# Attention and two mixture layers on one core: every stage cut into single steps, buffers and banks given out by the source, and the order of all engines and transfers fixed for the whole program

## The chip, the core and the metric

The kernel runs on one core of one Trainium2 chip, in one launch. The metric is the device time of that core in microseconds (us). The core has five engines that each take their instructions strictly in the order in which the program lists them: TensorE (PE, whose weight loads are the separate row PEld), VectorE (DVE), ScalarE (ACT), GpSimd (POOL) and SyncE (SP), which in this kernel only starts transfers. An instruction starts when those ahead of it on its engine allow it and when the semaphores that it waits for have come.

## The reference

Inputs are fp32: x is 8 batches x 8 heads x 512 x 64, state is 8 x 8 x 32 x 64. Cut to what matters:

```python
def _attn_ref(x, state):
    scores = scale * np.matmul(x, state.transpose(0, 1, 3, 2))
    a = softmax(scores);   xread = np.matmul(a, state)
    scores2 = scale * np.matmul(state, x.transpose(0, 1, 3, 2))
    a2 = softmax(scores2); sread = np.matmul(a2, x)
    return np.concatenate([xread, sread], axis=2)
def _moe_ref(x, w_in, w_out, g_ln):      # 512 -> 1024 -> 512
    h = x @ w_in
    sm = softmax(h);  solu = h * sm
    ln = (solu - mean) / np.sqrt(var + 1e-06) * g_ln
    return ln @ w_out
def _moe2_ref(x, w_in, w_out):           # 512 -> 2048 -> 512
    h = x @ w_in
    return np.maximum(0.01 * h, h) @ w_out
```

The rows between are 8 x (512 + 32) = 4352 tokens of 512 values.

## The kernel before, in words

The program has three stretches.

**The attention and the first layer, batch by batch.** For each batch b: `load_x` brings x into the one buffer `xn` (four transfers), `load_state` brings the state into `z`. `at_xT` transposes x on PE (tile `xt`, token `T`), `at_state` the state (`zt`, token `Z`), `at_scores` multiplies (`st`, token `S`) and starts the second softmax, `at_soft1` makes the first one (`ee`, token `U`), `at_a2T` and `at_sread` read the state's side (`a2t` and `sr`, tokens `A` and `R`), `at_a1T` the other (token `B`). `sw` (token `Y`, later `W`) is the state multiplied into the first layer's weights. `h1` is the first layer for 128 rows (token `h`, bank pair `h`), which ends in `solu_norm` (tiles `e(b, r)` of 128x1024 and columns of 128x1), `tr` transposes its result (`tr`), `x2` multiplies by w_out (`x`). Products are made of three fp32r matmuls on high and low halves (`mm3`), in batches 0 and 1 partly of plain fp32 ones. Weights are loaded raw (`a`, `b`), narrowed on DVE (`i`, `o`) and split into halves (`j`, `p`: ACT makes the high half, POOL the low one; the low halves of w_out are the instructions of line 245).

**The second layer's first pair of 512-token blocks (pair 0)**, chunk by chunk of the 2048 columns. `split_chunk` (token `d`) narrows a chunk of weights on DVE and has POOL make its low halves (`w2`, `wo2`, `misc`) and the four sums `ws`. `h2` (token `H`, tiles `C`, `gb`, `gc`) makes the hidden layer by a scheme of seven products, `out2` the output (`o`), and `h8`/`out8` (tokens `K`, `Q`, tiles `c8`, `g8`) do the same for the 256 rows of the state.

**Pairs 1 to 3**, from about 600 us on, are written step by step in `rest()` from the three tables HEAD, PATTERN and TURN; there `kept()` ties every instruction to the one before it on its engine.

Outside `rest()`, the string PROGRAM lists whole stages, one token each, and `emit` maps a token's letter to its function. Each stage issues all its instructions at once. `MANUAL` is False, so the tile scheduler then moves instructions on each engine by its own rules. Buffers that turn over are handed out by the pools: four banks under the one tag `p1`, two bank pairs under `p2`, three rows of 128x1024 under `t4`, sixteen small columns under `sm`.

Of the kernel before, what the change touches and what calls it, by code (L numbers as in the profile page):

```python
# [1 line left out]

# [18 lines left out]
P = 128  # L21
# [17 lines left out]

@with_exitstack  # L40
def attn_solu_leaky_kernel(
# [14 lines left out]
    nc = tc.nc  # L56
# [22 lines left out]
    def bank(name):  # L79
        return ps.tile([P, 512], F32, tag="p1", name=name, bufs=4)  # L80
# [4 lines left out]
    def bank2(name):  # L85
        return psb[0].tile([P, 1024], F32, tag="p2", name=name, bufs=2)
# [4 lines left out]
    def small(name, n=1):  # L91
        return sb.tile([P, 4], F32, tag="sm", name=name, bufs=16)[:, :n]

    def row(name):
        return slot("t4", [P, 1024], F32, name, bufs=3)
# [4 lines left out]
    ordered = {}  # L100

    def kept(ins):

        if "on" in ordered:
            e, last = ins.ins.engine, ordered["on"]
            if e in last:
                tc.add_manual_dep(
                    ins.ins, last[e],
                    mybir.DependencyInfo(mybir.DependencyClass.NoSync, mybir.DependencyReason.DATA),
                    reason="order",  # L110
                )
            last[e] = ins.ins.name
        return ins
# [18 lines left out]
    make_identity(nc, ident)  # L132
# [118 lines left out]
    def at_state(b):  # L251
        for g in range(2):
# [3 lines left out]
            )  # L256
            for m in range(2):
                i = 1 + (m + b) % 2
# [4 lines left out]
                else:  # L263
                    split(stq[:, 0, 2 * g + m, d], stq[:, 1, 2 * g + m, d], pt[:, c])
# [11 lines left out]
    def at_xT(b, hp):  # L276
# [3 lines left out]
        for r in range(NR):  # L280
            nc.tensor.transpose(
                pt[:, r * P : (r + 1) * P], xn[:, r, hp * P : (hp + 1) * P], ident
            )
        hi, lo = att["xT_hi"][:, hp, :], xT_lo[:, hp, :]
        if b in PLAIN_S:
            nc.scalar.activation(hi, pt, AF.Copy, scale=SCALE)
            return
        nc.scalar.activation(hi, pt, AF.Copy, scale=SCALE)
        nc.vector.scalar_tensor_tensor(lo, pt, SCALE, f32(hi), ALU.mult, ALU.subtract)

    def at_scores(b, g):
        st = bank(f"st{b}_{g}")
        for m in range(2):
# [8 lines left out]
            )  # L302
        nc.vector.transpose(s1[:, g, :], st)
# [16 lines left out]
    def at_soft1(b, g):  # L320
# [941 lines left out]
```

## Time and profile before

| what | value |
|---|---|
| median of 3 runs | 1175.23 us (1174.89 to 1177.4) |
| the profiled execution | 1174.46 us |
| its span from first to last instruction | 1172.6 us |
| mean granted clock of TensorE | 0.994 |
| instructions recorded | 16515 |

The profiled execution is the span and 1.9 us around it; the median lies 0.8 us above it. Times within a view are counted from the span's start. A line number names the line of the kernel that issued the instruction; "idle before, releaser" is the time that the engine stood still just before and the instruction that ended it.

### The profile page before, as it was taken

To read this page: it belongs to the slowest core of one execution; us is meant where nothing else is said; L and a number is where in the kernel's file an instruction comes from. 1 tells how busy PE (TensorE), PEld (TensorE's weight loads), DVE (VectorE), ACT (ScalarE), POOL (GpSimd) and SP (SyncE) were. 2 spreads that over 40 slices of the span, in tenths; PEclk is the share of its full clock that TensorE was granted. 3 is DMA by queue.
4 is the path that set the end of the run, shared out by engine and by line. 5 is a ranking of instruction groups with operands and counts; after the bars stand their busy time and mean duration, and the time that the engine had idled before them with its cause. 6 is when DMAs were issued, how large, how long until landed. Compare 5 with 4: busy or idle time off the path is not lost.

```text
span 1172.6 us, 16515 instructions
## 1 busy us (share of the span) xinstructions
PE 1133.9 (97%) x6192; PEld 950.1 (81%) x6192; DVE 902.6 (77%) x1406; ACT 542.8 (46%) x907; POOL 546.8 (47%) x411
## 2 busy tenths in 40 slices
PE   4979999999999999989999999999999999999998
PEld 2554688888888888768888889999899998899997
DVE  6787686886886678658887787878977768867787
ACT  4674655665565545453333434434543334443331
POOL 3233111201102032767666475887767466655453
PEclk9998999999999999999999999999999999999999
DMA  9530512342162163655664477675877476665442
GB/s 297 181 74 10 151 75 57 101 126 64 41 176 79 48 260 124 244 185 200 221 229 138 178 284 264 232 289 205 299 285 286 181 280 244 243 239 215 163 189 73
DMA packets 88376, 211.85 MB, mean 181 GB/s; under 512 B 41320, under 2 KB 49512, under 8 KB 79080
## 3 DMA queue, kind: packets, MB, share of 16 engines
q1 hardware_dynamic: 88296, 210.79, 50.7%
q8 instruction: 49, 0.80, 0.3%
q14 instruction: 31, 0.25, 0.1%
HBM read 151.00 MB, written 59.77 MB: 180 GB/s over the span
## 4 chain that ended last, share of the span: by engine, by line
PE 48%; DMA 2%; POOL 2%; issue 2%; DVE 1%; ACT 1%; POOLq 0%; DVEq 0%; SPq 0%
PE hX L118 4%; PE hX L119 4%; PE hX L120 4%; PE oX L120 4%; PE oX L118 4%; PE oX L119 4%; PE o L120 2%; PE o L119 2%; PE o L118 2%; PE hY L118 2%; PE hY L119 2%; PE hY L120 2%; PE oY L120 2%; PE oY L119 2%; PE oY L118 2%
## 5 line engine op out<-in xcount | busy, mean ns | idle before, releaser
L947 DVE TENSOR_TENSOR oacc<-oacc,oX 128x512 f32<-128x512 f32 x171 | 116.0, 682 | 52.5 <-PE oX L120 50.4
L118 PE MATMUL x<-ln,w_out_hi 128*128 128x512 f32 (+1 forms) x256 | 96.9, 378 | 0.0
L120 PE MATMUL x<-ln,w_out_lo 128*128 128x512 f32 (+1 forms) x256 | 96.4, 376 | 0.0
L119 PE MATMUL x<-ln,w_out_hi 128*128 128x512 f32 (+1 forms) x256 | 96.3, 376 | 0.0
L881 ACT COPY C<-hX 128x512 f32<-128x512 f32 x72 | 42.2, 586 | 115.4 <-PE hX L120 115.3
L118 PE MATMUL hX<-xbT,w 128*128 128x512 f32 x192 | 76.4, 398 | 0.8 <-ACT C L881 0.7
L119 PE MATMUL hX<-xbT,w 128*128 128x512 f32 x192 | 75.8, 395 | 0.3 <-POOL xbT L756 0.3
L120 PE MATMUL hX<-xbT,w 128*128 128x512 f32 x192 | 75.0, 391 | 0.0
L910 POOL TENSOR_TENSOR gc<-C,gc 128x512 fp32r<-128x512 f32 x35 | 47.2, 1351 | 39.3 <-ACT gc L906 31.9
L947 DVE TENSOR_TENSOR oacc<-oacc,oY 128x512 f32<-128x512 f32 x93 | 63.1, 682 | 3.0 <-PE oY L120 2.2
L910 POOL TENSOR_TENSOR gb<-C,gb 128x512 fp32r<-128x512 f32 x35 | 48.0, 1376 | 34.3 <-PE oX L120 22.5
L889 DVE SCALAR_TENSOR_TENSOR C<-C 128x512 f32<-128x512 f32 x72 | 63.3, 880 | 0.4
L886 DVE TENSOR_TENSOR C<-C,hY 128x512 f32<-128x512 f32 x48 | 32.9, 686 | 31.9 <-ACT C L881 27.1
L119 PEld LDWEIGHTS x<-ln,w_out_hi 128*128 128x128 f32 x256 | 48.2, 188 | 8.8
L120 PEld LDWEIGHTS x<-ln,w_out_lo 128*128 128x128 f32 x256 | 48.2, 188 | 8.8
L118 PEld LDWEIGHTS x<-ln,w_out_hi 128*128 128x128 f32 x256 | 48.2, 188 | 8.7
L334 POOL TENSOR_TENSOR ee<-ee,sm 128x512 f32<-128x512 f32 x16 | 18.1, 1134 | 78.2 <-DVE sm L333 38.9
L910 POOL TENSOR_TENSOR gb<-S,gb 128x512 fp32r<-128x512 f32 x27 | 43.8, 1629 | 19.9 <-ACT gb L906 16.3
L910 POOL TENSOR_TENSOR gc<-S,gc 128x512 fp32r<-128x512 f32 x26 | 39.8, 1539 | 24.8 <-ACT gc L906 20.4
L128 DVE TENSOR_TENSOR ln<-tr,ln 128x512 fp32r<-128x512 f32 x60 | 39.0, 682 | 10.6 <-ACT ln L127 10.2
L120 PEld LDWEIGHTS hX<-xbT,w 128*128 128x128 f32 x192 | 36.1, 188 | 8.2
L118 PEld LDWEIGHTS hX<-xbT,w 128*128 128x128 f32 x192 | 36.3, 189 | 7.2 <-ACT C L881 1.1
(982 smaller groups left out, 3956.6 us busy)
## 6 DMA issues: line engine op xcount, KB each, us to landing
w<-w2s SPq DMA_DIRECT2D x24, 1792.0 KB, 11.2
shared<-wo2s SPq DMA_DIRECT2D x24, 768.0 KB, 4.3
wi<-wsc SPq DMA_DIRECT2D x14, 1024.0 KB, 5.4
xs<-xo SPq DMA_DIRECT2D x34, 256.0 KB, 2.4
raw<-in_moe_w_in SPq DMA_DIRECT2D x8, 1024.0 KB, 6.1
raw<-in_moe_w_out SPq DMA_DIRECT2D x8, 1024.0 KB, 6.0
w2s<-w SPq DMA_DIRECT2D x8, 1024.0 KB, 5.3
wo<-wt2s SPq DMA_DIRECT2D x8, 1024.0 KB, 6.4
```

The lines of the kernel that those rows point to most:

```text
L118: kept(nc.tensor.matmul(o, ah, bh, start=start, stop=False, **kw))
L119: kept(nc.tensor.matmul(o, ah, bl, start=False, stop=False, **kw))
L120: kept(nc.tensor.matmul(o, al, bh, start=False, stop=stop, **kw))
L128: nc.vector.tensor_tensor(lo, src, f32(hi), ALU.subtract)
L334: nc.gpsimd.tensor_tensor(e3, e3, sm.unsqueeze(2).to_broadcast([P, 16, NS]), ALU.mult)
L881: kept(nc.scalar.copy({"e0": a11, "e2": a21, "e4": a22}[tok], q["X"]))
L886: kept(nc.vector.tensor_tensor(v, v, q["Z" if tok == "z1" else "Y"], ALU.add))
L889: kept(nc.vector.scalar_tensor_tensor(v, v, 0.01, v, ALU.mult, ALU.max))
L910: kept(e.tensor_tensor(t[:, 1], src, f32(t[:, 0]), ALU.subtract))
L947: kept(nc.vector.tensor_tensor(d, d, v, ALU.add))
```

## The change

Stages become generators that `yield` between steps, and each token of PROGRAM (now some 2,200 of them) issues only the next step of its stage. A wrapper stands around all five engines and ties each instruction to the one issued before it on the same engine, for the whole program, so that the order of the source is the order that runs; before, this held in `rest()` alone. The buffers and banks that turn over are no longer handed out by the pools: `take` gives a number from a list of free ones, each number is a tag of its own with one buffer, and `drop` gives it back after the last use. The single columns of `solu_norm` and the softmaxes become columns of one tile each (`sn`, `sa`, `mx`, `my`), `solu_norm` of the last rows is a stage of its own (`N`), and `split_chunk` has its parts 0 to 5. The first chunk of pair 1 is issued by tokens with a "/" in front. On every engine the number of instructions is as before (PE 5976, DVE 1372, ACT 823, POOL 414, SP 344); what `rest()` issues is in the same order as before.

```diff
+class InOrder:
+    def __init__(self, tc, engine):
+        self.tc, self.engine, self.last = tc, engine, None
+    def __getattr__(self, name):
+        call = getattr(self.engine, name)
+        def issue(*args, **kw):
+            done = call(*args, **kw)
+            if PINNED and self.last is not None:
+                self.tc.add_manual_dep(
+                    done.ins, self.last,
+                    mybir.DependencyInfo(mybir.DependencyClass.NoSync, mybir.DependencyReason.DATA),
+                    reason="order",
+                )
+            self.last = done.ins.name
+            return done
+        return issue
...
-    def bank(name):
-        return ps.tile([P, 512], F32, tag="p1", name=name, bufs=4)
+    free = {"t": [0, 1, 2], "p": [0, 1, 2, 3], "P": [0, 1], "ln": [0, 1, 2, 3], "wi": [0, 1]}
+    held = {}
+    def take(ring, name, uses=1):
+        held[name] = [ring, free[ring].pop(0), uses]
+        return f"{ring}{held[name][1]}"
+    def drop(name):
+        held[name][2] -= 1
+        if not held[name][2]:
+            ring, k, _ = held.pop(name)
+            free[ring].append(k)
+    def bank(name, uses=1):
+        return ps.tile([P, 512], F32, tag=take("p", name, uses), name=name, bufs=1)
...
     def at_scores(b, g):
...
+        yield
         nc.vector.transpose(s1[:, g, :], st)
-        nm = small(f"nm2_{b}_{g}")
+        yield
+        sa = slot(f"sa{b % 2}{g}", [P, 4], F32, f"sa{b}_{g}")
+        nm = sa[:, 0:1]
         nc.vector.tensor_reduce(nm, st, AX.X, ALU.max, negate=True)
-        s2 = small(f"s2_{b}_{g}")
+        yield
+        s2 = sa[:, 1:2]
         nc.scalar.activation(a2[:, g, :], st, AF.Exp, bias=nm, accum_out=s2)
...
-    with tc.manual_schedule() if MANUAL else ExitStack():
-        for u in PROGRAM.split():
-            emit[u[0]](*(int(v) for v in u[1:].split(".") if v))
+    stages = {}
+    for u in PROGRAM.split():
+        if u not in stages:
+            stages[u] = stage(u)
+        if stages[u] is not None:
+            next(stages[u], None)
-MANUAL = False
+PINNED = True
...
-    a0 a1 x0.0 T0.0 a2 a3 x0.1 T0.1 z0. i0 T0.2 i1 T0.3 Z0 z1. S0.1 Z1 S0.0 Y1.0 i3 Y0.0 i2 b0
+    a0 i0 i0 i0 i0 i0 z0. Z0.1 a1 x0.0 T0.0 Z0.0 a3 i1 i1 i1 Z0.0 Z0.0 z1. i1 T0.0 i1 T0.1 T0.1
+    a2 S0.0 x0.1 i3 Z0.1 Z1.1 i2 Z1.1 Z0.1 T0.3 Z1.1 T0.2 Y0.0.0 i3 i3 i3 T0.3 z2. i2 i2 i2 T0.2
```

Three places show how the orders differ. First PE at the very start: before, its first instructions up to the first `sw` (the eight transposes of `xt0_0` and `xt0_1` and most of those of `xt0_2` and `xt0_3` stand ahead of these rows).

```order
L281 MATMUL xt0_3_188<-ident_75,xn_91 128x128
L254 MATMUL zt0_0_194<-ident_75,z0_83 128x128
L254 MATMUL zt0_1_198<-ident_75,z0_83 128x128
L124 MATMUL st0_1_206<-xT_hi0_146,stp_94 128x512 x2
L254 MATMUL zt1_0_218<-ident_75,z1_84 128x128
L254 MATMUL zt1_1_222<-ident_75,z1_84 128x128
L124 MATMUL st0_0_226<-xT_hi0_146,stp_94 128x512 x2
L124 MATMUL sw1_0_0_238<-sw0_169,stp_94 128x512 x2
```

After, the same engine from its first instruction on:

```order
L51 MATMUL zt0_1_152<-ident_75,z0_83 128x128
L51 MATMUL xt0_0_160<-ident_75,xn_91 128x128 x4
L51 MATMUL zt0_0_165<-ident_75,z0_83 128x128
L51 MATMUL xt0_1_181<-ident_75,xn_91 128x128 x4
L51 MATMUL st0_0_188<-xT_hi0_159,stp_94 128x512 x2
L51 MATMUL zt1_1_199<-ident_75,z1_84 128x128
L51 MATMUL xt0_3_205<-ident_75,xn_91 128x128 x4
L51 MATMUL xt0_2_211<-ident_75,xn_91 128x128 x4
L51 MATMUL sw0_0_0_216<-sw0_141,stp_94 128x512 x2
```

The state's transposes and the first scores `st0_0`, which need only half of x, now stand ahead of the transposes `xt0_2` and `xt0_3` of the other half; the state's transfers were moved ahead of that half too.

Second DVE at batch 1's second softmax, before: `r2` is the factor that scales `q4`, which PE transposes as `a2t`; `nm(0, 3)`, `sm1` and `ee1` belong to other stages.

```order
L305 TENSOR_REDUCE nm2_1_0_463<-st1_0_459 128x1
L438 TENSOR_SCALAR e(0, 0)_430<-e(0, 0)_430,c2(0, 0)_444 128x1024
L331 TENSOR_REDUCE sm1_1_566<-ee1_493 128x16
L309 TENSOR_SCALAR r2_1_0_467<-s2_1_0_465 128x1
L305 TENSOR_REDUCE nm2_1_1_481<-st1_1_477 128x1
...
L311 TENSOR_SCALAR q4_93<-q4_93,r2_1_0_467 128x512
L309 TENSOR_SCALAR r2_1_1_485<-s2_1_1_483 128x1
L415 TENSOR_REDUCE nm(0, 3)_511<-h0_3_506 128x1
L310 RECIPROCAL r2_1_1_485<-r2_1_1_485 128x1
L333 RECIPROCAL sm1_1_566<-sm1_1_566 128x16
L311 TENSOR_SCALAR q4_93<-q4_93,r2_1_1_485 128x512
```

After, with `sa1_0` and `sa1_1` as the tiles of the same columns:

```order
L51 STREAM_TRANSPOSE q4_93<-st1_0_419 128x512
L51 TENSOR_REDUCE sa1_0_436<-st1_0_419 128x1
L51 SCALAR_TENSOR_TENSOR e(0, 0)_422,sn(0, 0)_414<-h0_0_372,e(0, 0)_422 128x1024
...
L51 RECIPROCAL sa1_0_436<-sa1_0_436 128x1
L51 STREAM_TRANSPOSE q4_93<-st1_1_444 128x512
L51 TENSOR_REDUCE sa1_1_450<-st1_1_444 128x1
...
L51 TENSOR_SCALAR q4_93<-q4_93,sa1_0_436 128x512
L51 TENSOR_TENSOR ee1_454<-q4_93,mx1_1_455 128x512
...
L51 TENSOR_SCALAR sa1_1_450<-sa1_1_450 128x1
L51 RECIPROCAL sa1_1_450<-sa1_1_450 128x1
L51 TENSOR_SCALAR q4_93<-q4_93,sa1_1_450 128x512
```

Both maxima now come right behind their transposes, and `nm(0, 3)` and the scaling of `e(0, 0)` no longer stand among them.

Third POOL at the end of the first layer, before: `gb` and `gc` are the low halves of the hidden layer of pair 0, `g8_0` that of the state's rows, the others make weights of chunks 1 and 2.

```order
L849 TENSOR_TENSOR gb_3963<-C_3728,gb_3963 128x1024
L855 TENSOR_TENSOR gb_3963<-C_3728,gb_3963 128x1024
L590 TENSOR_TENSOR w2_0_1_4111<-wn1_0_4104,w2_0_1_4111 128x1024
...
L849 TENSOR_TENSOR gc_4125<-C_3728,gc_4125 128x1024
L855 TENSOR_TENSOR gc_4125<-C_3728,gc_4125 128x1024
L590 TENSOR_TENSOR w2_0_2_4357<-wn2_0_4350,w2_0_2_4357 128x1024
L1022 TENSOR_TENSOR g8_0_4259<-c8_0_4256,g8_0_4259 128x512
L601 TENSOR_TENSOR w2_0_2_4357<-ws2_4360,w2_0_2_4357 128x1024
```

After:

```order
L51 TENSOR_TENSOR gb_3743<-C_3538,gb_3743 128x1024
...
L51 TENSOR_TENSOR w2_0_1_3924<-ws1_3925,w2_0_1_3924 128x1024
L51 TENSOR_TENSOR misc_3964<-wn1_1_3839,misc_3964 128x1024
L51 TENSOR_TENSOR gb_3743<-C_3538,gb_3743 128x1024
...
L51 TENSOR_TENSOR g8_0_4109<-c8_0_4104,g8_0_4109 128x512
L51 TENSOR_TENSOR w2_0_2_4084<-ws2_4085,w2_0_2_4084 128x1024
L51 TENSOR_TENSOR gc_3975<-C_3538,gc_3975 128x1024 x2
```

`g8_0` now stands ahead of both `gc`, and weight work stands between the two `gb`.

## Rows read from the trace of the kernel before

**Rows 1.** The page's part 1: busy us (share of the span) xinstructions.

```profile
PE 1133.9 (97%) x6192; PEld 950.1 (81%) x6192; DVE 902.6 (77%) x1406; ACT 542.8 (46%) x907; POOL 546.8 (47%) x411
```

**Rows 2.** Stretches: us; busy of PE, PEld, DVE, ACT, POOL; clock; DMA share, GB/s.

```profile
9.00:29.00 20.00, 14.25 (x35) 6.60 (x36) 16.50 (x24) 10.63 (x23) 5.80 (x2) 1.00 0.94 305
29.00:117.00 88.00, 79.77 (x289) 45.40 (x288) 69.91 (x135) 53.25 (x96) 26.95 (x23) 0.94 0.30 89
117.00:469.00 352.00, 350.89 (x1804) 288.96 (x1803) 266.65 (x514) 201.25 (x362) 65.09 (x89) 1.00 0.34 108
469.00:541.00 72.00, 65.45 (x329) 54.18 (x328) 49.82 (x48) 33.33 (x44) 52.90 (x29) 0.98 0.64 220
600.00:1172.60 572.60, 564.55 (x3460) 505.59 (x3458) 451.07 (x632) 216.20 (x349) 352.32 (x237) 1.00 0.60 226
```

**Rows 3.** Waits of PE, 0 to 117 us: total, times, longest.

```profile
PE xt L281 <- DMA xn<-in_x: 14.0, 2, 9.0
PE a2t L343 <- DVE r L309: 3.4, 1, 3.4
PE st L119 <- DVE xT_lo L289: 2.4, 1, 2.4
PE st L124 <- ACT xT_hi L286: 1.6, 1, 1.6
PE tr L490 <- DVE e(0, 2)_627 L438: 0.7, 1, 0.7
```

**Rows 4.** Waits of PE, 469 to 541 us.

```profile
PE o L120 <- POOL g L1022: 3.1, 1, 3.1
PE o L118 <- ACT g L1021: 1.0, 1, 1.0
PE h L119 <- DVE misc L1002: 0.9, 1, 0.9
```

**Rows 5.** Three stretches at half clock, columns as in rows 2.

```profile
68.95:72.36 3.41, 3.41 (x16) 3.06 (x16) 3.41 (x6) 2.04 (x4) 1.14 (x1) 0.50 0.00 0
89.43:96.26 6.83, 6.14 (x19) 4.53 (x20) 4.86 (x6) 2.00 (x4) 6.70 (x3) 0.50 0.00 0
509.27:512.68 3.41, 2.88 (x7) 2.30 (x8) 2.94 (x2) 0.98 (x2) 2.80 (x2) 0.50 0.54 192
```

**Rows 6.** Timeline of PE: start, us, instruction [idle before <-releaser].

```profile
8.96 2.30 PE L281 MATMUL xt<-ident,xn 128*128 128x128 f32 x8 [8.96 <-DMA xn<-in_x]
...
16.27 2.45 PE L281 MATMUL xt<-ident,xn 128*128 128x128 f32 x8 [5.01 <-DMA xn<-in_x]
...
36.35 1.04 PE L343 MATMUL a2t<-ident,q 128*128 128x128 f32 x8
...
40.88 3.68 PE L355 MATMUL sr<-ee,xn 128*128 128x64 f32 x32
44.40 6.23 PE L124 MATMUL h<-sw,a1T 128*128 128x512 f32 x14
```

**Rows 7.** Issues of SP, 40 to 55 us, and their landing over 43 to 52 us.

```profile
43.93 2.94 SPq L171 DMA_DIRECT2D xn<-in_x  x4
xn<-in_x SPq DMA_DIRECT2D x4, 256.0 KB, 4.4
```

**Rows 8.** Timeline of DVE, 60 to 92 us.

```profile
68.68 1.22 DVE L415 TENSOR_REDUCE nm(0, 3)_511<-h 128x1 f32<-128x1024 f32 x1
78.97 0.80 DVE L438 TENSOR_SCALAR e(0, 3)_513<-e(0, 3)_513,c2(0, 3)_527 128x1024 f32<-128x1024 f32 x1
89.28 2.33 DVE L438 TENSOR_SCALAR e(0, 2)_627<-e(0, 2)_627,c2(0, 2)_641 128x1024 f32<-128x1024 f32 x1
```

**Rows 9.** Timeline of POOL, at 86 us and at the boundary.

```profile
86.39 9.74 POOL L245 TENSOR_TENSOR w_out_lo<-w_out_f,w_out_hi 128x1024 fp32r<-128x1024 f32 x4
503.82 2.37 POOL L855 TENSOR_TENSOR gc<-C,gc 128x1024 fp32r<-128x1024 f32 x1 [2.24 <-ACT gc L854]
...
508.46 1.28 POOL L1022 TENSOR_TENSOR g<-c,g 128x512 fp32r<-128x512 f32 x1
```

More of the change, by code (lines that the diff above doesn't have):

```diff
@@ L85, in bank2, with row @@
     def bank2(name):
-        return psb[0].tile([P, 1024], F32, tag="p2", name=name, bufs=2)
+        return psb[0].tile([P, 1024], F32, tag=take("P", name), name=name, bufs=1)
     def bank1(tag, name):
         return psb[0].tile([P, 512], F32, tag=tag, name=name, bufs=1)
[L91 to L95, printed above, removed]
+    def row(name, uses=1):
+        return slot(take("t", name, uses), [P, 1024], F32, name)
     xs = [dr.tile([P, ND, S if j < B else HALF], F32, name=f"xs{j}") for j in range(B + 1)]
[L100 to L113, printed above, removed]
     def mm3(o, ah, al, bh, bl, start, stop, more=False):
         kw = {"skip_group_check": True} if more else {}
-        kept(nc.tensor.matmul(o, ah, bh, start=start, stop=False, **kw))
-        kept(nc.tensor.matmul(o, ah, bl, start=False, stop=False, **kw))
-        kept(nc.tensor.matmul(o, al, bh, start=False, stop=stop, **kw))
+        nc.tensor.matmul(o, ah, bh, start=start, stop=False, **kw)
+        nc.tensor.matmul(o, ah, bl, start=False, stop=False, **kw)
+        nc.tensor.matmul(o, al, bh, start=False, stop=stop, **kw)
     def mm1(o, a, b, start, stop):
@@ L203, in load_w_in @@
         if k == 0:
-            raws["i"] = [slot("ln", [P, 2, FF, 2], U32, f"raw_in{i}", bufs=4) for i in range(2)]
+            raws["i"] = [slot(take("ln", f"raw_in{i}", 2), [P, 2, FF, 2], U32, f"raw_in{i}") for i in range(2)]
         nc.sync.dma_start(raws["i"][k // 2][:, k % 2], w_in[k * P : (k + 1) * P])
@@ L225, in load_w_out @@
         if k == 0:
-            raws["o"] = [slot("ln", [P, 2, 2 * DM, 2], U32, f"raw_out{i}", bufs=4) for i in range(2)]
+            raws["o"] = [slot(take("ln", f"raw_out{i}", 2), [P, 2, 2 * DM, 2], U32, f"raw_out{i}") for i in range(2)]
         nc.sync.dma_start(
@@ L380, in sw_of, with at_sw1 @@
         return sw[b]
-    def at_sw1(b, g):
-        for n in range(2):
+    def at_sw1(b, g, n):
+        for _ in (0,):
             c = slice(n * 512, (n + 1) * 512)
@@ L456, in h1 @@
                 )
-        solu_norm((b, r), hp_)
+        yield
+        yield from solu_norm((b, r), hp_)
     hs = []
     def h1s(k):
-        if k == 0:
-            hs.extend(bank2(f"hs{r}") for r in range(2))
         for r in range(2):
+            if k == 0:
+                if r:
+                    yield
+                hs.append(bank2(f"hs{r}"))
             for n in range(2):
@@ L725, in line @@
     def line(n, p):
-        return row(f"{n}_{p}").rearrange("p (k t) -> p k t", k=2)
+        return row(f"{n}_{p}", 2 if n in ("T1", "T2") else 1).rearrange("p (k t) -> p k t", k=2)
     def xpart(p, n):
@@ L917, in out2s @@
         new = n in ("A11", "S1") or (n == "A12" and c == 0)
-        if q == 0:
-            if n == "A12" and c == 0:
-                oq[p, tag] = [bank1(t, f"oz{p}_{t}") for t in "JZ"]
-            elif new:
-                oq[p, tag] = [bank(f"o{tag}{p}_{c}_{u}") for u in range(2)]
-        else:
+        if new:
+            u = f"o{tag}{p}_{c}_{q}"
+            oq[p, tag, q] = bank1("JZ"[q], u) if n == "A12" else bank(u)
+        if q:
             ring.append(a)
-        pt = oq[p, tag][q]
+        pt = oq[p, tag, q]
         for k in range(2):
@@ L991, in rows8 @@
         load_x8()
-        split_x8()
+        yield
+        yield from split_x8()
     def load_x8():
@@ L1118, in split_srs @@
         t = slot("q6", [P, 2, NHP, B * NS], F32R, "srs")
-        split(t[:, 0], t[:, 1], srT)
-        return t[:, 0], t[:, 1]
+        yield from split(t[:, 0], t[:, 1], srT)
+        srs.extend((t[:, 0], t[:, 1]))
     srs = []
@@ L1148, in attn_solu_leaky_kernel @@
         "d": split_chunk,
-        "s": lambda: srs.extend(split_srs()),
+        "s": split_srs,
         "D": first_x2,
         "E": second,
-        "H": lambda p, c, i: (h2(p, c, i), [step(t, p, c) for t in (AFTER.get(i, "") if p else "").split()]),
+        "H": h2,
         "O": out2,
```

583 lines of the change are left out of this document (407 added, 176 removed).

## The prediction

> **What bounds the kernel now.** I read the busy times first [rows 1]: PE has 97% of the span, the next engine 77%, so a gain can only come from time in which PE stands still or works slowly. The table of stretches [rows 2] says where that is. From 117 to 469 us PE is idle for 352.00 − 350.89 = 1.1 us: nothing is left there. From 600 us on it is idle for 572.60 − 564.55 = 8.1 us, but that part keeps its order. What is open lies at two places: the start (9.0 us before the first matmul [rows 6], 20.00 − 14.25 = 5.8 us from 9 to 29 us, 88.00 − 79.77 = 8.2 us from 29 to 117 us) and the boundary between the layers (72.00 − 65.45 = 6.6 us from 469 to 541 us).
>
> Then the waits, by name. In the start [rows 3] PE waits 14.0 us for x (9.0 and 5.0, the two idle times of [rows 6]), and 3.4 + 2.4 + 1.6 + 0.7 = 8.1 us for DVE and ACT: the first 3.4 us before `a2t` of batch 1, 2.4 us before the scores of batch 2, 1.6 us before those of batch 1, 0.7 us before a `tr`. At the boundary [rows 4] it waits 3.1 us for POOL's `g`, 1.0 for ACT's `g` and 0.9 for `misc`, 5.0 us in the rows shown. Last the clock: at the 3.4, the 2.4 and the 3.1 us wait, from just ahead of their end on, PE runs at 0.50, its lower level of 1.2 GHz, for 3.41, 6.83 and 3.41 us [rows 5], 1.00 (2.4 GHz) around them. Matmuls at half clock do half the work, so these stretches cost about half their PE time: 3.41/2 + 6.14/2 + 2.88/2 = 6.2 us.
>
> So the most that an order could return is 9.0 + 5.8 + 8.2 + 6.6 + 6.2 = 35.8 us without what `rest()` holds; the 9.0 us are the first transfers themselves, which leaves 26.8 us.
>
> **The change part by part.**
>
> *Tying each instruction to the one before.* Engines run their lists in order anyway, and counts are equal on all five, so the ties themselves are worth nothing: no instruction is added that could cost, and the merged columns only join tiles. What is bought or sold is the order. From 600 us on it is unchanged: 0 there. What I put at nothing there is covered as before by PE's 564.55 us of work.
>
> *The start, 0 to 29 us.* The scores `st0_0` and the first state transposes now run between the two halves of x, in the 5.0 us [rows 6] in which PE stood still. That is about 2 matmuls of 128x512 in plain fp32; by the fourteen of [rows 6] (6.23/14 = 0.45 us a record, two records each) 4 records or 1.8 us, with some transposes (1.04/8 = 0.13 us each) about 2.4 us filled. Against it, eight state transfers now go ahead of the second half of x. They are small, and each issue holds SP for about 2.94/4 = 0.74 us [rows 7]. If the issues were the limit the second half would come 6 us later, but the DMA share is 0.94 in that stretch [rows 2], so it is the bytes that count, and these are few: I take 1 us late. Bounds −4 to +4, value +1.5.
>
> *29 to 117 us.* The wait of 3.4 us: the last scaling of `q4` came behind the maximum `nm(0, 3)`, 1.22 us [rows 8], and behind a scaling of `e(0, 0)` (0.80 by its like [rows 8]) and two operations on `ee1`/`sm1` (0.7 each, by the same engine's 128x512 forms, which I read as a bit under the 0.80). Out of order's way that is 1.22 + 0.80 + 1.4 = 3.4 us ahead of it: the wait goes. The second and fourth waits (2.4 and 0.7) come from POOL. At 86.39 us POOL begins four subtractions of w_out one after the other, 9.74 us [rows 9], and inside them the scaling of `e(0, 2)` takes 2.33 us where its like takes 0.80 [rows 8]. In the new order these four stand as one, two and one with other stages between, so that no DVE run is stretched three times in a row. The Trainium skill, "SBUF — State Buffer", section "Who interferes with whom", says that GpSimd and VectorE share one port pair as an exclusive lock, and that the loser blocks entirely; the 2.33 us against 0.80 agree with it. By that rule a move does not remove the 9.74 us of overlap, it only picks other victims. That is the ground of the rival below on POOL; in the sum, the 2.4 + 0.7 count in full. The 1.6 us for ACT's `xT_hi`: the new order puts the transposes of `xt1` together instead of spread over `h0`, with `st1_0` soon behind the two that it needs, so part of the wait stays; I count half, 0.8. Sum 3.4 + 2.4 + 0.7 + 0.8 = +7.3, bounds 0 and 8.2 (all of the stretch's idle time). Where the stall goes: DVE, with 69.91 of 88.00 us busy [rows 2], is next; 18 us of slack lie spread over the stretch, so the wait need not come back, but it may.
>
> *The clock.* Two of the three half-clock stretches lie in the start, just behind the 3.4 us and the 2.4 us waits [rows 3, 5]. If those waits go I take the clock to stay up: 3.41/2 + 6.14/2 = 4.8 us, of which I count 4.6. Bounds 0 and 4.8.
>
> *The next x.* `xn` has one buffer, so x of a batch can only be fetched when the last `sr` of the batch before has read it. In the kernel before, the four transfers started with `sr` running (40.88 to 44.56 us [rows 6]; issues 43.93 to 46.87, landing 4.4 us after issue [rows 7]), so x is there about 46.87 + 4.4 = 51.3 us at the latest, some 6 to 7 us behind the last `sr`. In the new order PE has, between the last `sr` and the first `xt` of the next batch, in batch 1 the transposes and the `h1_2` and half `h1_0`, 12 records at 0.45 = 5.3 us and 13 transposes at 0.13 = 1.7 us, 7.0 us in all; for the other batches I counted 6.5 to 15. That is just covered. Cost 0, and if the cover is gone a microsecond or two in each of seven batches.
>
> *117 to 469 us.* It has 1.1 us idle: nothing to win, and a hand-set order may make new waits. Bounds −10 and +1, value −3.
>
> *The boundary.* POOL is the engine waited for. There the low half `g8_0` (1.28 us) came behind `gc` (2.37) and `w2_0_2` (2.36, the time between the two rows less waits) [rows 9], and PE stood for 3.1 us [rows 4]. In the new order `g8_0` stands ahead of both `gc`. That takes 2.37 us at least from its start, and its consumer `o` stands later on PE too: 3.1 + 1.0 + 0.9 = 5.0 us, and the 2.88/2 = 1.4 us of the third half-clock stretch [rows 5]. `gc` behind it is 2 x 2.4 us later in POOL's list by one 1.28 us operation, and its first use on PE comes some 9 us after. I count +6.5 (6.4 summed, and 0.1 of smaller waits). Bounds −3 and +8.
>
> **Sum:** 1.5 + 7.3 + 4.6 − 3 + 6.5 = 16.9 us. The profiled execution of before took 1174.46 us (span 1172.6 and 1.9 around it), so 1157.6 us. The median of the runs is 0.8 us above the profiled one; on that scale **1158.3 us**. A measurement of this kernel can tell about 0.2%, 2.4 us, from no change; 16.9 is seven times that.
>
> **The rivals.**
>
> *Half of it, chance 0.20.* DVE is the limiter one step below PE: in 29 to 117 us it is busy for 69.91 us in a fixed list. If each wait that goes comes back shorter at the next thing PE needs from DVE, or one of the four POOL subtractions stretches another DVE run on PE's path by the same 1.5 us, start and boundary return half of 1.5 + 7.3 + 4.6 + 6.5 = 19.9 us, less 1.5 for new waits: 1175.2 − 8.5 = 1166.7. For it: 88.00 − 69.91 = 18 us of slack is spread thin. Against it: PE's waits there are four single events, not a steady lag.
>
> *No difference, 0.07.* The order as printed moves, but what PE waits for is the same data through the same chain, and the clock falls at other places. Then 1175. Against it: the 9.74 us of POOL in one piece is plainly split.
>
> *Slower, by the x cover, 0.07.* One place: the fetch of the next x behind the last `sr`. If it takes 9.5 us instead of the 6 to 7, because the new order sends more before it in the queue, PE stands 2.5 us in each of seven batches = 17.5 us, which eats the 16.9; a clock that falls after each (3.41/2 = 1.7 us, seven times 12) makes it 1175.2 − 16.9 + 17.5 + 12 = 1188. The point from which it decides is 9.5 us of fetch; [rows 7] shows 7.4 from the first issue. Before has no wait for x behind 29 us, which is against it.
>
> *More, 0.05.* The start hides nearly all of the 5.0 us and 117 to 469 us loses nothing: 1175.2 − 26.8 = 1148.5.
>
> **How the numbers follow.** The forecast, a gain of 12 to 23 us, has 0.61. Its own range is 1152 to 1164. The half-gain case takes the upper end to 1168, the greater gain the lower to 1148; left out are no difference, slower, and the tails: about 0.2. Range 1148 to 1168. Faster by over 0.2%: 0.61 + 0.20 + 0.05 = 0.86; within: 0.07; slower: 0.07.
>
> **What would show it.** Right: PE's first wait for x of 9 us stays, the second is shorter; no wait of PE above 1 us from 29 to 117 us, and clock 1.00 throughout; POOL's subtractions of w_out apart, and DVE's scalings of `e` at 0.8 us; no wait of `o` for POOL's `g`; waits from 117 to 469 us below 4 us; everything behind pair 1's start as long as before. Wrong: a `xt` in some batch that waits for DMA; PE waiting for DVE in many short pieces; idle time from 117 to 469 us above 10 us.

## The result and the profile after

The changed kernel takes 1156.14 us (median of 4 runs, 1155.37 to 1157.69), the kernel before 1175.06 in the same session: a ratio of 0.9836, 95% interval 0.9819 to 0.9853. The forecast was 1158.3 us, with 1148 to 1168 as the range. The profiled execution took 1156.16 us; its span is 1154.4 us, 18.2 less than before. Recorded instructions all carry line 51 now, the wrapper's call, so groups are read by their tiles.

The table of stretches of the changed kernel, columns as in [rows 2]. Places in the program come 16 to 18 us earlier behind the boundary, so its stretches end at 453, 523 and 582 us where those of before ended at 469, 541 and 600:

```profile
0.00:9.00 9.00, 0.44 (x1) 0.18 (x1) 1.76 (x3) 2.44 (x3) 3.87 (x11) 1.00 0.84 274
9.00:29.00 20.00, 17.84 (x45) 8.36 (x46) 19.24 (x28) 12.94 (x26) 3.15 (x1) 1.00 1.02 337
29.00:117.00 88.00, 87.75 (x346) 50.99 (x345) 76.76 (x154) 59.62 (x111) 23.12 (x24) 1.00 0.36 112
117.00:453.00 336.00, 334.07 (x1732) 278.33 (x1731) 259.30 (x488) 191.86 (x345) 69.13 (x88) 1.00 0.35 105
453.00:523.00 70.00, 70.00 (x379) 60.44 (x378) 41.92 (x47) 36.01 (x50) 44.55 (x26) 1.00 0.57 192
...
582.00:1154.40 572.40, 559.83 (x3413) 498.28 (x3411) 450.79 (x634) 214.88 (x347) 354.43 (x236) 1.00 0.62 233
```

Idle time is the stretch less PE's busy time. From 29 to 117 us it fell from 8.2 to 0.25 us, at the boundary from 6.6 to 0. From 0 to 29 us it is 8.56 + 2.16 = 10.7 us; before it was 9.0 + 5.8 = 14.7. In the last stretch it rose, from 572.60 − 564.55 = 8.1 us to 572.40 − 559.83 = 12.6: a loss that the prediction did not have.

The waits of PE over the whole program, the three largest:

```profile
PE zt L51 <- DMA z<-in_state: 6.9, 1, 6.9
PE xt L51 <- DMA xn<-in_x: 5.3, 5, 2.3
PE oX L51 <- POOL gc L51: 3.4, 2, 3.1
```

Nothing of [rows 4] is left, and of [rows 3] only the wait for the first transfers, now spread over `zt` and `xt`, and 0.2 us of the 1.6 for `xT_hi`. Of the five waits for x four, 3.3 us, lie in the start, and one, 1.9 us, in batch 4. New is 3.1 us before an `oX` that waits for POOL's `gc`. The clock is at its lower level in one stretch behind that wait, where [rows 5] showed three; this is the table of stretches for it:

```profile
699.51:702.92 3.41, 3.41 (x13) 2.83 (x12) 2.67 (x3) 0.45 (x1) 3.41 (x3) 0.50 1.07 449
```

How the new wait comes about is read in two timelines of the changed kernel, POOL's and SP's:

```profile
682.85 1.74 POOL L51 TENSOR_TENSOR gb<-C,gb 128x512 fp32r<-128x512 f32 x1
693.14 0.74 POOL L51 TENSOR_TENSOR wd<-wf 128x256 f32<-128x256 f32 x1 [8.55 <-DMA wf<-wf2s]
...
697.26 2.95 POOL L51 TENSOR_TENSOR gc<-C,gc 128x512 fp32r<-128x512 f32 x2
```

```profile
678.20 0.34 SPq L51 DMA_DIRECT2D out<-oacc  x1
680.51 0.32 SPq L51 DMA_DIRECT2D wt2s<-misc  x1
681.11 0.57 SPq L51 DMA_DIRECT2D out<-oacc  x1
681.78 0.84 SPq L51 DMA_DIRECT2D wf<-wf2s  x1
```

POOL stands for 8.55 us until `wf` lands at 693 us, then makes four sums `wd` of it, and only then `gc`, for which PE waits. SP issues that `wf` last, behind the last output rows of pair 0 and a store of weights, each of which first waits for its data. SP's timeline of the kernel before at the same work has it the other way round:

```profile
677.44 1.63 SPq L638 DMA_DIRECT2D wf<-wf2s  x1
...
688.90 0.34 SPq L988 DMA_DIRECT2D out<-oacc  x1
```

There only what `rest()` issues was tied, and this load is the first transfer of it; the scheduler was free to place pair 0's output rows behind it.

### The profile page after: what moved, and what is told of

Its sections match the earlier page's. It is cut to its first block, busy times and chain, and to the rows that moved or that the text cites. A ratio compares the mean times of both kernels' runs of the same rounds, so it can differ in the third digit from the quotient of the medians.

```text
span 1154.4 us, 16468 instructions
## 1 busy us (share of the span) xinstructions
PE 1128.9 (98%) x6192; PEld 945.8 (82%) x6192; DVE 895.7 (78%) x1406; ACT 540.7 (47%) x907; POOL 540.2 (47%) x411
## 4 chain that ended last, share of the span: by engine, by line
PE 89%; DMA 4%; DVE 3%; issue 1%; POOL 1%; ACT 0%; POOLq 0%; SPq 0%; DVEq 0%; ACTq 0%
PE x L51 17%; PE hX L51 14%; PE oX L51 10%; PE h L51 10%; PE o L51 8%; PE hY L51 7%; PE oY L51 5%; PE hZ L51 3%; PE tr L51 3%; PE sr L51 2%; PE oZ L51 2%; PE st L51 2%; PE sv L51 1%; DVE C L51 1%; PE sw L51 1%
## 5 line engine op out<-in xcount | busy, mean ns | idle before, releaser
L51 PE MATMUL x<-ln,w_out_hi 128*128 128x512 f32 (+1 forms) x512 | 153.8, 384 | 0.0
L51 PE MATMUL hX<-xbT,w 128*128 128x512 f32 x576 | 149.9, 395 | 1.5 <-ACT C L51 1.2
L51 PE MATMUL h<-sw,a1T 128*128 128x512 f32 x352 | 103.6, 436 | 0.0
L51 POOL TENSOR_TENSOR gc<-C,gc 128x512 fp32r<-128x512 f32 (+1 forms) x43 | 69.3, 1614 | 50.2 <-ACT gc L51 25.5
L51 POOL TENSOR_TENSOR gb<-C,gb 128x512 fp32r<-128x512 f32 (+1 forms) x43 | 69.8, 1629 | 45.9 <-ACT gb L51 23.6
L51 DVE SCALAR_TENSOR_TENSOR C<-C 128x512 f32<-128x512 f32 (+1 forms) x88 | 82.7, 940 | 0.6
L51 PEld LDWEIGHTS h<-sw,a1T 128*128 128x128 f32 x352 | 64.1, 188 | 23.2 <-issue 11.0
L51 DVE TENSOR_TENSOR oacc<-oacc,o 128x512 f32<-128x512 f32 x70 | 45.7, 681 | 21.6 <-PE o L51 21.3
L51 ACT CAST ln<-tr 128x512 fp32r<-128x512 f32 x60 | 34.5, 588 | 35.3 <-PE tr L51 35.2
L51 PE MATMUL hX<-xbB,w 128*128 128x512 f32 x192 | 50.9, 401 | 0.0
L51 PE MATMUL hY<-xbB,w 128*128 128x512 f32 x192 | 49.7, 394 | 0.4 <-DVE C L51 0.4
```

Of the source, the lines that this page charges most:

```text
L51: done = call(*args, **kw)
```

## The experiments

All are the changed kernel with the edit shown; the last has the two edits before it together. Tokens are given as they stand in PROGRAM, and lists are cut to the lines that change. Times are medians, to be held against 1156.1 us. Runs of one kernel lie 2 to 6 us apart here, so a difference of about 3 us is read from the trace and not from the time alone.

**Ties taken away, wholly and in part.**

```diff
-PINNED = True
+PINNED = False
```

> The changed kernel without the ties: steps, buffers and banks as in the change, but the scheduler may move instructions again on every engine (on DVE and SP its order then differs in most places). If the order is what pays and ties are free, as the prediction has it, the gain goes back in large part: 1165 to 1176 us. Rival: the division into steps and the buffers given out by the source carry the gain, and the scheduler keeps close enough to the source: 1155 to 1159 us.

Measured: 1241.96 us, 1.0572 (1.0557 to 1.0586) of before. Both expectations were too low by far. The two largest waits of PE:

```profile
PE hX L51 <- ACT C L51: 11.7, 5, 5.8
PE o L51 <- DVE oacc L51: 11.6, 5, 3.8
```

Since this also frees the part from pair 1 on, which was tied before the change, a second kernel keeps ties there alone:

```diff
     def rest():
+        global PINNED
+        PINNED = True
+        for n in vars(nc).values():
+            n.last = None
...
-PINNED = True
+PINNED = False
```

> The changed kernel with ties in the part written step by step alone, as before the change; steps, buffers and banks ahead of it as in the change, in the scheduler's order. Theory: fixed order ahead of that part is the whole gain, and what the scheduler makes of the divided source there costs at least as much as before: 1172 to 1185 us (the kernel without any tie lost 17 us more of PE's time than the changed one up to 560 us, and some of the clock). Rival: steps and buffers carry a part of the gain: 1158 to 1168 us.

Measured: 1206.57 us, 1.026 (1.0244 to 1.0277), again above both expectations. So the changed source without its order ahead of pair 1 is 31 us slower than the kernel before, and that order is worth 50 us on top of it. Which of the steps, the buffers and the new list of tokens the scheduler does badly with, no run separates. The table of stretches shows that the loss against the changed kernel lies at the start and, most of it, from 453 to 640 us, where PE is idle for 8.9 and 12.0 us and the clock's mean falls to 0.97 and 0.96:

```profile
29.00:117.00 88.00, 79.75 (x300) 45.21 (x300) 79.87 (x152) 60.37 (x108) 35.34 (x29) 0.96 0.31 94
...
453.00:560.00 107.00, 98.06 (x512) 83.37 (x511) 76.09 (x74) 49.19 (x67) 63.93 (x36) 0.97 0.54 187
560.00:640.00 80.00, 68.03 (x316) 55.61 (x314) 54.64 (x63) 28.06 (x36) 49.35 (x29) 0.96 0.53 179
```

**The start undone.** z goes behind x again, with what uses it.

```diff
-    a0 i0 i0 i0 i0 i0 z0. Z0.1 a1 x0.0 T0.0 Z0.0 a3 i1 i1 i1 Z0.0 Z0.0 z1. i1 T0.0 i1 T0.1 T0.1
-    a2 S0.0 x0.1 i3 Z0.1 Z1.1 i2 Z1.1 Z0.1 T0.3 Z1.1 T0.2
+    a0 i0 i0 i0 i0 i0 a1 x0.0 T0.0 a3 i1 i1 i1 i1 T0.0 i1 T0.1 T0.1 a2 x0.1 i3 i2 T0.3 T0.2 T0.3
+    T0.2 z0. z1. Z0.1 Z0.1 Z0.1 Z0.0 Z0.0 Z0.0 Z1.1 Z1.1 Z1.1 S0.0
```

> The changed kernel with the old start: the state's eight first transfers go behind the second half of x, and the state's transposes and st0_0 behind the transposes of x. The prediction's term of 1.5 us for the new start makes this 1157.6 us. Rival, by the idle time of PE from 0 to 29 us in the two traces (14.7 us before, 10.7 after): the start was worth 4 us, 1160 us.

Measured: 1159.29 us (1155.95 to 1161.43), 3.2 us more, with ranges that overlap; the span is 2.7 us longer. Its wait for x from 0 to 40 us is about what it was before the change, against 6.9 us for the state and 3.3 for x with the new start:

```profile
PE xt L51 <- DMA xn<-in_x: 13.4, 2, 8.9
```

What the start is worth is read better from the time at which PE reaches the first `sr` of batch 0, here, in the changed kernel and in the one with x of batch 4 first (further down):

```profile
36.60 1.89 PE L51 MATMUL sr<-ee,xn 128*128 128x64 f32 x16
32.58 1.89 PE L51 MATMUL sr<-ee,xn 128*128 128x64 f32 x16
36.26 1.89 PE L51 MATMUL sr<-ee,xn 128*128 128x64 f32 x16
```

The last two have the same order on every engine up to there. So have the eight other kernels below that keep all ties, and over these ten the time lies between 32.58 and 36.26 us, 34.5 in the mean. It goes with how long PE waits for the second half of x and whether the clock falls behind that wait: in eight of the ten profiles it is at its lower level there, for 3.4 us in six and for 6.8 in two. The profile of the changed kernel is one of the two without. For the slowest of the ten, the wait and the row of the table of stretches:

```profile
19.19 2.56 PE L51 MATMUL xt<-ident,xn 128*128 128x128 f32 x8 [3.04 <-DMA xn<-in_x]
```

```profile
18.16:24.99 6.83, 5.80 (x13) 2.94 (x14) 5.64 (x8) 2.65 (x6) 0.00 (x0) 0.50 0.74 236
```

So the start is worth between 0.3 and 4.0 us, about 2 in the mean, against the one profile of the old start. The rival's 4 is the gain of the fastest start of the ten, and these runs don't tell the sum's 1.5 from 3.

**The 3.4 us wait before `a2t`: PE's list or DVE's?** First PE's alone, `h0_3` behind the transposes:

```diff
-    o0 h0.3 S1.0 U1.1 Z2.1 U1.0 U1.1 h0.0 h0.3 S1.1 h0.1 S1.1 U1.0 U1.0 h0.1 A1.0 A1.0 A1.1 A1.1
+    o0 S1.0 U1.1 Z2.1 U1.0 U1.1 h0.0 S1.1 h0.1 S1.1 U1.0 U1.0 h0.1 A1.0 A1.0 A1.1 A1.1 h0.3 h0.3
```

> The changed kernel with one move on PE alone: the four matmuls of h0_3 go behind the transposes a2t of batch 1 instead of ahead of them; DVE's list stays. The prediction says that the wait of 3.4 us went because DVE's list no longer holds nm(0, 3) and the scalings ahead of the last scaling of q: then PE waits nothing here, 1156 us. Rival: PE's own list covers the wait with h0_3; DVE's last scaling ends at 56.9 us in the profile and PE would be there at about 54.1: a wait of 2.8 us, and a stretch at half clock behind it for 1.7 us more: 1159 to 1161 us.

Measured: 1159.11 us (1157.28 to 1160.99), as the rival has it. PE's timeline has the wait again, in two pieces, with no half clock behind it:

```profile
57.97 0.30 PE L51 MATMUL a2t<-ident,q 128*128 128x128 f32 x1 [0.74 <-DVE q L51]
59.99 0.98 PE L51 MATMUL a2t<-ident,q 128*128 128x128 f32 x7 [1.72 <-DVE q L51]
```

Then DVE's alone. A first try delayed the scaling behind its readers, so that `a2t` read `q` before its last scaling:

```diff
-    S1.1 U1.0 U1.0 h0.1 A1.0 A1.0 A1.1 A1.1 h0.0 j1 t0.0.0 t0.0.0 U1.1 U1.1 h0.2 h0.1 t0.1.0 h0.3
+    U1.0 U1.0 h0.1 A1.0 A1.0 A1.1 A1.1 h0.0 j1 t0.0.0 t0.0.0 U1.1 U1.1 h0.2 h0.1 t0.1.0 h0.3 S1.1
```

> The changed kernel with one move on DVE alone: the last scaling of q of batch 1 goes behind the maximum nm(0, 3) and what stands before it, about 4.2 us of DVE work later; PE's list stays, which reaches these transposes 0.6 us after the scaling ends now. The prediction's step: a wait of about 3.6 us comes back, with up to 1.7 us for the clock: 1160 to 1161.5 us. Rival: PE's list has enough room behind (softmax chains run ahead of need), and nothing comes back: 1156 to 1157 us.

Measured: 1155.5 us (1155.15 to 1158.56). With the dependency gone there was nothing to wait for, so this run tells nothing on the question. The second try brings the other work forward instead:

```diff
-    h0.1 S1.1 U1.0 U1.0 h0.1 A1.0 A1.0 A1.1 A1.1 h0.0 j1 t0.0.0 t0.0.0 U1.1 U1.1 h0.2 h0.1 t0.1.0
-    h0.3
+    h0.1 h0.1 h0.0 U1.1 h0.1 h0.3 S1.1 U1.0 U1.0 A1.0 A1.0 A1.1 A1.1 j1 t0.0.0 t0.0.0 U1.1 h0.2
+    t0.1.0
```

> The changed kernel with one move on DVE alone: ahead of the last scaling of q of batch 1 now stand the maximum nm(0, 3), the scalings of e(0, 0) and e(0, 1) and the sum of ee, about 4.1 us of work; PE's list stays, which reaches these transposes 0.6 us after the scaling ends now. The prediction's step (DVE's list alone made the wait): a wait of about 3.5 us comes back, with up to 1.7 us for the clock: 1159.5 to 1161.5 us. Rival: nothing comes back, since the chain runs ahead of PE's need: 1156 to 1157 us.

Measured: 1160.76 us (1158.28 to 1161.62), in the range of the prediction's step. PE's timeline and, below it, the stretch behind the wait, at half clock:

```profile
62.19 0.98 PE L51 MATMUL a2t<-ident,q 128*128 128x128 f32 x7 [2.79 <-DVE q L51]
```

```profile
63.50:66.80 3.30, 3.30 (x5) 1.21 (x5) 1.05 (x3) 2.29 (x4) 2.04 (x2) 0.50 0.00 0
```

So either move alone brings a wait of 2.5 to 2.8 us. In the new order both are needed: DVE's list is shorter ahead of the last scaling, and PE has `h0_3` to do meanwhile. That is not yet how the old wait came about; see the next section.

**POOL's four subtractions in one piece.** Four more of the same size, which the output does not need, at the place where they stood before the change:

```diff
+    def pool4():
+        w = raws["w"][:, 0:2, :]
+        for _ in range(4):
+            nc.gpsimd.tensor_tensor(w_out_lo[:, 6:8, :], w, w, ALU.subtract)
...
-    T2.2 o3 T2.0 t0.3.1 h0.2 t0.3.0 T2.0 h0.2 t0.2.0 T2.1
+    T2.2 o3 T2.0 t0.3.1 h0.2 t0.3.0 T2.0 h0.2 t0.2.0 T2.1 !
```

> The changed kernel with four subtractions of 128x1024 more on POOL, one after the other (9.7 us of work that the output does not need), ahead of the transposes of batch 2, where four of them stood in one piece before the change. The prediction's step (this piece made the waits of 2.4 and 0.7 us, by what it does to DVE): waits of about 3 us come back, and up to 3 us of clock: 1159 to 1162 us. Rival: what removed the waits is the order of PE and DVE there, and POOL's piece costs under 1 us: 1156 to 1157 us.

Measured: 1158.37 us (1157.41 to 1163.44), between the two expectations; the traces decide. The timelines of POOL, DVE and PE:

```profile
71.98 8.55 POOL L51 TENSOR_TENSOR w_out_lo<-w_out_f 128x1024 fp32r<-128x1024 f32 x4
```

```profile
72.51 1.47 DVE L51 TENSOR_SCALAR sn(0, 2)_535<-sn(0, 2)_535 128x2 f32<-128x2 f32 x1
74.01 2.46 DVE L51 TENSOR_SCALAR e(0, 2)_564<-e(0, 2)_564,sn(0, 2)_535 128x1024 f32<-128x1024 f32 x1
```

```profile
76.62 0.63 PE L51 MATMUL tr<-ident,e(0, 2)_564 128*128 128x128 f32 x4 [2.14 <-DVE e(0, 2)_564 L51]
```

Inside POOL's piece the scaling of `e(0, 2)` takes 2.46 us (0.81 in the changed kernel), much as the 2.33 of [rows 8], and PE waits 2.1 us for it; 3.4 us at half clock follow. Of the two waits of before the `tr` one came back, larger; that of `st` for `xT_lo` did not.

**The boundary's 3.1 us wait.** POOL's list alone, `g8_0` (the last K0 step) behind the first `gc` and `w2_0_2`:

```diff
-    K0 d2.0.3 K0 H0.1.5 d2.0.1 O0.0.1.1 K1 K1 K1 H0.2.0 H0.2.1 Q0.0 H0.2.0 H0.1.6 H0.2.1 d2.1.0
-    d2.0.3 d3.0.0 H0.2.2 Q0.1 O0.0.0.0 d2.0.4 d2.0.5 H0.1.5
+    K0 d2.0.3 H0.1.5 d2.0.3 H0.1.5 K0 d2.0.1 O0.0.1.1 K1 K1 K1 H0.2.0 H0.2.1 Q0.0 H0.2.0 H0.1.6
+    H0.2.1 d2.1.0 d3.0.0 H0.2.2 Q0.1 O0.0.0.0 d2.0.4 d2.0.5
```

> The changed kernel with POOL's old order at the boundary: g8_0 stands behind the first gc and the low half of w2_0_2, 4.8 us of POOL work later; PE's list stays. The prediction gave the 3.1 us wait and 1.4 us of clock to POOL's order: then 1160.6 us. Rival: PE's list, which uses g8_0 only 4.2 us after POOL has it, removes the wait by itself: a wait of 0.6 us at most, 1156 to 1157 us.

Measured: 1158.83 us, with wide runs (1156.34 to 1162.14), so the time falls between the expectations. The profiled execution is the fastest of the five; its span, 1154.6 us, is that of the changed kernel, and of the boundary's wait this came back:

```profile
PE o L51 <- POOL g L51: 0.8, 1, 0.8
```

POOL's and PE's list together, with the first `o8_0` (Q0.0) ahead of `h8_1`, `hX` and `hZ` as well:

```diff
-    H0.1.5 K0 d2.0.1 O0.0.1.1 K1 K1 K1 H0.2.0 H0.2.1 Q0.0
+    H0.1.5 K0 Q0.0 d2.0.1 O0.0.1.1 K1 K1 K1 H0.2.0 H0.2.1
```

> The changed kernel with both halves of the boundary's wait undone: g8_0 behind the first gc and the low half of w2_0_2 on POOL, and the first o8_0 ahead of h8_1, hX and hZ on PE. Theory: POOL's and PE's order each give cover (4.8 us and 5.6 us of work against 4.2 us of slack now), and only with both gone does a wait come back: about 6 us, with up to 1.7 us for the clock: 1161 to 1164 us. Rival: other work slides in and no more than 1 to 2 us come back: 1157 to 1158 us.

Measured: 1164.39 us (1160.68 to 1167.01), 8.3 us more, at the upper end of the theory. The wait, in the slowest of the six runs:

```profile
PE o L51 <- POOL g L51: 6.2, 1, 6.2
```

So it was not POOL's order by itself; PE's later use covers almost all of POOL's 4.8 us.

**The new wait at 699 us.** `wf2` is issued before the last output rows:

```diff
     def load_wf(c):
+        if c in wf:
+            return
...
-    Q7.0 /7.uc /8.V /8.m6
+    Q7.0 /7.uc /8.V /9.U /8.m6
```

> The changed kernel with one transfer moved: the load of wf2 is issued before the last output rows of pair 0 instead of behind them. Theory: the new wait of 3.1 us at 699 us and the half clock behind it come from fixed order on SP, which puts these output rows (and what they wait for) ahead of wf2; then 3.1 + 1.7 us go, 1151.4 us. Rival: the transfer is late because the DMA is busy, or POOL's sums are late for another reason: 1155 to 1157 us.

Measured: 1152.26 us (1151.57 to 1155.17), 0.9813 (0.9799 to 0.9828) of before, 3.9 us less than the changed kernel, and no run of the one lies in the range of the other. SP issues the load 4.4 us earlier, and POOL's sums are done before `gc` is wanted; the wait of 3.1 us and the half clock behind it are gone. SP and POOL in the trace of this run, which is the slowest of the four:

```profile
677.33 2.67 SPq L51 DMA_DIRECT2D wf<-wf2s  x1
682.12 0.34 SPq L51 DMA_DIRECT2D out<-oacc  x1
```

```profile
690.84 0.75 POOL L51 TENSOR_TENSOR wd<-wf,wd 128x256 f32<-128x256 f32 x1
695.90 1.29 POOL L51 TENSOR_TENSOR gc<-C,gc 128x512 fp32r<-128x512 f32 x1 [4.32 <-ACT gc L51]
```

**The wait for x of batch 4.** In the changed kernel PE's transposes wait once behind the start for x. Its timelines of PE and SP there:

```profile
181.15 1.20 PE L51 MATMUL xt<-ident,xn 128*128 128x128 f32 x9 [1.93 <-DMA xn<-in_x]
```

```profile
165.68 0.92 SPq L51 DMA_DIRECT2D wi<-wsc  x2
168.84 7.42 SPq L51 DMA_DIRECT2D xn<-in_x  x4
```

Two reloads of 1 MB go just ahead of x, and x takes 181.15 − 168.84 = 12.3 us from the first issue to the use of the last piece. The edit moves them behind it (`x4.` is unchanged; only its neighbours shown):

```diff
-    X1.2 w2.0 B3.0 B3.0 w2.1 h2.3
+    X1.2 B3.0 B3.0 h2.3
...
-    t2.0.0 x4. Z5.0
+    t2.0.0 x4. w2.0 w2.1 Z5.0
```

> The changed kernel with two transfers moved: the reloads of two first-layer weights (1 MB each) go behind the four transfers of x of batch 4 instead of ahead of them. Theory: they are why batch 4's transposes wait 1.9 us for x; then 1154.2 us. Rival: the reloads are then late for the state's product of batch 2 and the wait only changes its place: 1156 us or more.

Measured: 1155.36 us (1154.25 to 1157.19). No wait for x is left behind the start, nor one for the reloads; the time is 0.8 us less, which these runs can't tell from none. The profiled execution is even 1.0 us longer than that of the changed kernel: it is the one whose start came out 3.7 us later, as shown above.

**Both moves of transfers.**

> The changed kernel with both moves of transfers, wf2 early and x of batch 4 first. If both theories hold the gains add: 3.1 + 1.7 + 1.9 us, 1149.5 us, faster than both kernels. If either falls, 1151 to 1156 us.

Measured: 1152.27 us (1149.46 to 1152.86), 0.9804 (0.979 to 0.9818) of before: faster than both kernels, and equal to the one with `wf2` alone within the spread. Both waits are gone in its trace, but the 1149.5 us of the added gains did not come; its profiled execution has 3.4 us at half clock in the start. That the move of x is worth something in time is not shown.

## Why the prediction was right, and where its terms were not

The total, 1156.1 against 1158.3, and the sign are right, and so are the places of the gains. The terms err more than the total. In span, from the two profiles:

| term | predicted | measured | how |
|---|---|---|---|
| start, 0 to 29 us | +1.5 | +4.0 | idle 14.7 to 10.7; by the first `sr` 0.3 to 4.0 over ten profiles |
| waits, 29 to 117 us | +7.3 | +8.0 | idle 8.2 to 0.25 |
| 117 us to the boundary | −3 | −0.8 | idle 1.1 to 1.9 |
| boundary, waits | +5.1 | +6.6 | idle 6.6 to 0 |
| clock, three stretches | +4.6 and +1.4 | +5.0 | PE busy 1133.9 to 1128.9, the new stretch included |
| from pair 1 on | 0 | −4.5 | idle 8.1 to 12.6 |

The measured column adds up to 18.3, the span's 18.2. Two errors cancel: the gains were put 6 us too small in sum, and a loss of 4.5 us, with 1.7 us of half clock counted in the clock's row, was left out. That the total comes within 2.2 us is in part luck.

**The step that failed** is "From 600 us on it is unchanged: 0 there". The order of what `rest()` issues is unchanged, but not what stands ahead of it on SP; and `rest()` begins only with the load of `wf2`, so the first chunk of pair 1 ahead of it got a new order too. Tying the whole program put pair 0's output rows in front of `wf2`; the run with the load moved shows that cause, and that it cost 3.9 us. Of the 4.5 us of idle time 3.1 are this wait; the rest is in pieces below 1 us, which no run takes apart. The prediction asked what is queued on SP for the start and for x, but not here, and took unchanged work in a stretch for unchanged waits.

**The start.** I counted 2.4 us filled and 1 us lost. PE filled more: the four records of `st0_0` took 3.75 us, not 1.8, at a granted clock of 1.00, where those of `st0_1` took 1.88 a little later.

```profile
12.86 3.75 PE L51 MATMUL st<-xT_hi,stp 128*128 128x512 f32 x4 [0.17 <-issue]
21.40 1.88 PE L51 MATMUL st<-xT_hi,stp 128*128 128x512 f32 x4
```

Time filled by slow work is not all gained, and the half clock that most of the profiles have behind the second half of x was no term of the sum. By the ten profiles +1.5 is within what the start is worth.

**The wait of 3.4 us** was forecast to go, and went, but its lines were misread. The prediction added up what stands ahead of the last scaling of `q4`, `nm(0, 3)` included. PE's and DVE's timelines of the kernel before:

```profile
68.85 0.58 PE L343 MATMUL a2t<-ident,q 128*128 128x128 f32 x2 [3.35 <-DVE r L309]
69.22 1.91 PE L490 MATMUL tr<-ident,e(0, 0)_430 128*128 128x128 f32 x8
70.93 1.49 PE L343 MATMUL a2t<-ident,q 128*128 128x128 f32 x6
```

```profile
65.52 0.81 DVE L438 TENSOR_SCALAR e(0, 0)_430<-e(0, 0)_430,c2(0, 0)_444 128x1024 f32<-128x1024 f32 x1
...
68.22 0.48 DVE L311 TENSOR_SCALAR q<-q,r 128x512 f32<-128x512 f32 x1
...
68.68 1.22 DVE L415 TENSOR_REDUCE nm(0, 3)_511<-h 128x1 f32<-128x1024 f32 x1
...
70.03 0.46 DVE L311 TENSOR_SCALAR q<-q,r 128x512 f32<-128x512 f32 x1
```

The wait ended at 68.85 us, behind the first scaling, which is done at 68.70; `nm(0, 3)` and the last scaling come later. The transposes that need the last scaling stand behind eight `tr` on PE and did not wait. So what made the wait stands ahead of 68.22 us, the scaling of `e(0, 0)` and three reductions of 0.68 us among it, and that the prediction's sum is 3.4 too is luck. In the new order nothing stands on PE between the transposes of the two halves, so that the last scaling counts there; undoing PE's or DVE's part brings 2.5 or 2.8 us of wait and costs 3.0 or 4.6 us. The prediction named DVE's list alone. The same holds for **the boundary**: POOL's list undone alone returns a wait of 0.8 us, together with PE's 6.2. The prediction did mention the later use on PE, but rested the term on POOL. (The 2.36 us that it gives for `w2_0_2` is 2.27 by its two rows.)

**POOL's piece** was right in mechanism. The Trainium skill, "SBUF — State Buffer", section "Who interferes with whom", gives GpSimd and VectorE an exclusive port pair, and limits it to some VectorE instructions, `tensor_scalar` in its two-port modes among them and `tensor_reduce` not. The 2.46 us against 0.81 for the same scaling beside a piece of 8.55 us agree with it, and so does a reduction that takes 1.23 us in that piece as without it. The prediction left the limit out when it said that a move only picks other victims. That rival did not come: in the changed kernel no wait of PE behind DVE from 29 to 117 us is left. Only the `tr` part of the two waits was reproduced. For the 2.4 us of `st` for `xT_lo` the trace of before shows the same cause: `c2(0, 2)`, 128x2, takes 2.31 us inside the piece, where its like takes 0.23, and `xT_lo` stands right behind it.

```profile
86.45 2.31 DVE L437 TENSOR_SCALAR c2(0, 2)_641<-cf(0, 2)_632,rs(0, 2)_638 128x2 f32<-128x2 f32 x1 [0.71 <-POOL rs(0, 2)_638 L435]
88.68 0.68 DVE L289 SCALAR_TENSOR_TENSOR xT_lo<-xt,xT_hi 128x512 fp32r<-128x512 f32 x1
```

In the changed order `xT_lo` stands further behind. That its wait did not come back for this reason is argued; no run separates it.

**The rival by x cover** was seen once, in batch 4, at 1.9 us and for the reason that it gave: more ahead of x in the queue (12.3 us of fetch against the 9.5 from which it was to decide). It needed seven batches to turn the sign, and had one. A `xt` that waits for a transfer was the first of the prediction's signs of being wrong, and it came; so small, it did not make the total wrong.

**The ties** "are worth nothing" can hold for their own cost only, which no run shows by itself. As the way to get the order they are worth 50 us ahead of pair 1, since the scheduler makes a slower order of the changed source (1206.6 us) than of the one before (1175).

## What to carry to other kernels

When order is fixed, read it on every queue, that of the transfers first: a store that waits for its data holds up each load behind it, and shows up as a wait two engines further on. When a wait goes, ask both lists, that of the engine that was late and that of the one that waited, since cover may come from either. Stages divided into steps, without the order fixed, gave the scheduler a source that it ordered worse: 31 us here. And hold a gain that is read from one profile against the profiles of other kernels that have the same order there: the start's 4.0 us was the best of ten.

## What the runs showed that I had not expected

Runs of the changed kernel's variants lie further apart than those of before: 2.9 to 6.3 us from lowest to highest in four to six runs each, where nine to eleven of before lie within 1.8 to 4.8. A part of it shows in the profiles, at two places where the order is the same and the time is not. One is the start, 3.7 us from the fastest to the slowest of ten. The other is x of batch 4: among the nine profiles of kernels that keep all ties and have the two reloads ahead of it the wait is missing in two (the second try on DVE's list, and POOL's four subtractions), and between 1.1 and 2.6 us in seven. The four longest, 2.02 to 2.61 us, were followed by 3.4 us at half clock, some 1.7 us more; those of 1.09, 1.93 and 2.00 were not. This is the table of stretches of the kernel with `wf2` early, behind a wait of 2.49 us that ended at 183.52 us:

```profile
184.00:187.40 3.40, 3.40 (x13) 2.92 (x12) 2.83 (x4) 2.12 (x4) 0.00 (x0) 0.50 0.00 0
```

That these two places are the whole of the spread is only argued; the moves of transfers that take the second wait away were run five and four times, too few to show a narrower spread.
